# Attention and swish MLP on one core: value phase of batches 0 and 1 pipelined, beta read later, batch 1's attention front moved into pass 2 of slab 0, later norms moved into pass 1

## The chip, the core and the metric

The kernel runs on one core of a Trainium2 chip. The metric is the device time of one execution in microseconds. The engines are called as in the profile: PE (TensorE matmuls; PEld its weight loads), DVE (VectorE), ACT (ScalarE), POOL (GpSimd) and SP (the queue that issues most DMAs). Each engine works through its own instruction queue in order; semaphores tie the queues together.

## What is computed

For 8 batches with 8 heads, 576 positions and 64 channels, a softmax of q over its channels and of k over the positions gives a linear attention; its output goes through an MLP with a swish that has a slope for each hidden channel.

```python
q_s = exp(q - max(q, -1));  q_s /= sum(q_s, -1)
k_s = exp(k - max(k, 2));   k_s /= sum(k_s, 2)
kv  = einsum('bhsd,bhse->bhde', k_s, v)
x   = einsum('bhsd,bhde->bhse', q_s, kv)     # to 4608 tokens x 512
h   = x @ w_in                               # 512 -> 2048
g   = h * sigmoid(beta * h)
out = g @ w_out                              # 2048 -> 512
```

## The kernel before

**Slabs.** The 576 positions of a batch are split into 512 and a remainder of 64. Slab t (0 to 7) is the 512 tokens of batch t; slab 8 is the eight remainders together. For each slab `pass1_tile` runs 16 times: four matmuls of 128x512 (`PS<-XT,WIN`), then ScalarE's Silu with scale beta into `GT`. `pass2_group` then forms the output with 64 matmuls (`PS<-WOUT,GT`), copied to `O2S` and stored. beta's reciprocal is folded into `WOUT` (`scale_wout`).

**Attention of a batch.** It gives `XT`, the left side of pass 1. Head pairs (hp, four of them) are the unit:
- ScalarE's exps: `exp_q` (EQ), `exp_k` (EK), and `exp_kr`, `exp_qr` for the remainders (EKR, EQR).
- `norm_main`: sum of EQ over channels (QS, line 306), reciprocal (QI, 307) and product in place (308); `norm_rem` does it for EQR.
- `t_steps`: four transposes of EQ by a matmul with the identity (line 343), copied to `QT` (363). `tr_steps` does it for EQR (QTR).
- `cast_v` and `cast_vr`: v to bf16 with a column of ones (VB, VR).
- `kv_steps`: EK times VB, five matmuls for a pair, with the sum of EK as column 129; its reciprocal is `RC`, and `kvd` makes `KVD` = product x RC x a mask (380). `ksum` is the sum alone.
- `out_step`: `QT` times `KVD` (`out_mm`), copied to `XT` (417). `outr_steps` does it for the remainders of two batches into `XT8`.

**Order.** The program is written out by hand: `add` appends an operation to its engine's queue and derives its semaphore waits from the tiles and PSUM banks that it touches. In a slab's passes a `tick` runs after each matmul, and `todo` holds steps of the next batch's attention with the tick from which they may go (1 to 64 in pass 1, 65 to 128 in pass 2). PSUM has eight banks: pass 1 rotates through 0 to 2 (HB), pass 2 through 3 and 4 (in slab 0: 3 to 6), attention through 5 to 7 (MB). Batches 0 and 1 have no pass of an earlier slab that could hold all of their attention: `attn_now` runs it at once, for batch 0 in the head of the kernel, for batch 1 between slab 0 and slab 1. There `warm` fills gaps with matmuls whose result nobody reads. Batch 2's attention (`attn_late`) lies in pass 2 of slab 1, batch b's (3 to 7) over both passes of slab b - 1.

**Loads.** SP loads batch 0 (q, beta, k, v); POOL issues eight loads of `WIN`, the first when the last of k has landed; SP then waits for the sixth of them, loads w_out into staging tiles, then batch 1, then batch 2 and so on. POOL also does some norm products and most casts of v.

Of the kernel before, what the change touches and what calls it, by code (L numbers as in the profile page):

```python
# [17 lines left out]
DFF = 2048  # L18
NF = DFF // 128
NM = DM // 128  # L20
# [133 lines left out]
def bass_efficient_attn_shen__then__act_swish_beta_kernel(  # L154
# [12 lines left out]
    with ExitStack() as es:  # L167
# [243 lines left out]
        def out_step(b, hp, pool=MB):  # L411
            i = b % 2

            def one():
                bk = bank(pool)
                out_mm(b, hp, bk)
                add(DVE, lambda e: e.tensor_copy(XT[i][:, hp, :], PS[bk][:, :]),  # L417
                    r=[("ps", bk)], w=[("xt", i, hp)], bank=[bk])
            return [one]
# [34 lines left out]
        def attn(b):  # L454
            s = t_steps(b, (0, 1)) + t_steps(b, (2, 3))
            if b % 2:
                s += tr_steps()
            s += kv_steps(b, (0, 1)) + kv_steps(b, (2, 3))
            for hp in range(NHP):
                s += out_step(b, hp)  # L460
            if b % 2:
                s += outr_steps(b)
            return s

        def attn_late(b):
            s = []
            for hps in ((0, 1), (2, 3)):
                s += t_steps(b, hps) + kv_steps(b, hps)
            for hp in range(NHP):
                s += out_step(b, hp)  # L470
            return s
# [8 lines left out]
        def attn_now(b, pool, wbank, wn, mid):  # L480
            i = b % 2

            def go(steps):
                for s in steps:
                    s()

            def ksum(hp):
                for j in range(5):
                    l, r_, ke, kv, ko = kv_rows(b, hp, j)
                    mm(PS[kb][:, hp:hp + 1], l, r_[:, 128:129], j == 0, j == 4, r=ke + ko,  # L490
                       w=[("ps", kb)], bk=kb)

            exp_q(b)
            for hp in range(NHP):
                norm_main(b, hp, 1, POOL if hp % 2 else DVE)
            mid()
            kb = bank(pool)
            go(t_steps(b, (0,), pool, ACTE))
            warm(wn[0], wbank)
            exp_kr(b, (b % 2,))  # L500
            exp_k(b, 0, 1)
            go(t_steps(b, (1,), pool, ACTE))
            warm(wn[1], wbank)
            exp_k(b, 1, 1)
            ksum(0)
            exp_k(b, 2, 1)
            ksum(1)
            go(t_steps(b, (2,), pool, ACTE))
            warm(wn[2], wbank)
            exp_k(b, 3, 1)  # L510
            ksum(2)
            cast_v(b, 0, ACTE)
            cast_v(b, 1, ACTE)
            go(t_steps(b, (3,), pool, ACTE))
            warm(wn[3], wbank)
            ksum(3)
            cast_v(b, 2, ACTE)
            cast_v(b, 3, ACTE)
            add(DVE, lambda e: e.reciprocal(RC[i][:, :], PS[kb][:, 0:NHP]), r=[("ps", kb)],
                w=[("rc", i, hp) for hp in range(NHP)], bank=[kb])  # L520
            for hp in range(NHP):
                bk = bank(pool)
                for j in range(5):
                    l, r_, ke, kv, ko = kv_rows(b, hp, j)
                    mm(PS[bk][:, 0:128], l, r_[:, 0:128], j == 0, j == 4, r=ke + kv,
                       w=[("ps", bk)], bk=bk)
                kvd(b, hp, bk, 0)
                warm(wn[4], wbank)
                go(out_step(b, hp, pool))
# [24 lines left out]
        HEAD = (1, 2, 3, 4, 5, 6, 7)  # L554
        warm(8, 0)
        bb = bank(HEAD)
# [11 lines left out]
        wgate = []  # L568

        def load_win():  # L570
            for c in range(8):
                a = bass.AP(win_h, 256 * c, [[DFF, 128], [128 * DFF, NM], [1, 256]])
                add(POOL, lambda e, c=c, a=a: e.dma_start(WIN[:, :, 256 * c:256 * c + 256], a),
# [162 lines left out]
```

## Time and profile before

| | |
|---|---|
| median of 3 runs | 328.35 us (327.58 to 328.57) |
| the profiled execution, its own time | 327.24 us |
| its span | 325.4 us |
| PE busy | 293.5 us (90%) |
| ACT, DVE, POOL busy | 166.6, 122.5, 36.6 us |
| DMA | 44.30 MB, mean 136 GB/s |

In a timeline a row is: start and duration in us, engine, line of the kernel, operation, output tile <- input tiles, sizes, count of merged instructions, and in brackets how long the engine had been idle before and what ended that. "SPq" and "POOL ... DMA" rows are issues of a DMA, not its transfer. In the table by stage a row gives the stretch and its length, then each engine's busy time with its count, the granted clock of TensorE, the mean busy share of the DMA engines and GB/s. PEclk on the page is the granted clock in tenths, for 40 equal slices of the span.

### The profile page before, as it was taken

What the parts mean: (1) busy time and instruction counts of PE and PEld (TensorE: products, weight loads), DVE (VectorE), ACT (ScalarE), POOL (GpSimd) and SP (SyncE); (2) the same over time, 40 slices, a digit from 0 to 9 for tenths busy, and PEclk for the clock granted to TensorE, in tenths of its full rate; (3) what the DMA queues carried; (4) which work ended last, traced back from release to release, by engine and by line L of the source; (5) the groups of instructions that cost most, each with busy time, mean ns of one, the idle gap of its engine ahead of it and who ended that gap; (6) DMA issues with size and microseconds to landing.
All of it is one profiled execution on the core that took longest, in us unless ns stands there. A gap on an engine that the chain in (4) does not pass through costs nothing.

```text
span 325.4 us, 3908 instructions
## 1 busy us (share of the span) xinstructions
PE 293.5 (90%) x1569; PEld 139.6 (43%) x1600; DVE 122.5 (38%) x238; ACT 166.6 (51%) x252; POOL 36.6 (11%) x63
## 2 busy tenths in 40 slices
PE   4769992879949999999989989999899999999995
PEld 1334441434425455445535534454355444444442
DVE  1650435251344935910681167107812520010011
ACT  4557407837980569067806780678066018406700
POOL 4460001200073303010200110000000000000000
PEclk9999998799989999999999999999999999999999
DMA  7799999999079952960493000300030002003012
GB/s 213 207 155 255 375 307 286 282 317 254 4 254 250 343 151 69 341 172 2 136 283 131 0 2 2 129 0 2 0 130 2 0 32 99 0 0 131 0 51 78
DMA packets 46098, 44.30 MB, mean 136 GB/s; under 512 B 13808, under 2 KB 42496, under 8 KB 45056
## 3 DMA queue, kind: packets, MB, share of 16 engines
q1 hardware_dynamic: 41536, 41.43, 42.0%
q0 software_dynamic: 4224, 2.10, 5.0%
q10 hardware_dynamic: 320, 0.52, 0.4%
q8 instruction: 12, 0.20, 0.3%
q14 instruction: 6, 0.05, 0.1%
HBM read 36.71 MB, written 9.44 MB: 142 GB/s over the span
## 4 chain that ended last, share of the span: by engine, by line
PE 78%; DVE 13%; ACT 2%; POOL 2%; issue 2%; DMA 1%; SPq 1%; POOLq 0%; DVEq 0%
PE PS L345 76%; DVE QS L306 3%; DVE EQ L308 3%; DVE XT L417 2%; PE PS L343 2%; DVE KVD L380 2%; DMA BT<-in_moe_beta_dram 1%; DVE O2S L604 1%; DVE QI L307 1%; POOL EQ L308 1%; ACT L280 1%; POOL VR L331 1%; SPq L251 1%; ACT EQ L280 0%; ACT O2S L604 0%
## 5 line engine op out<-in xcount | busy, mean ns | idle before, releaser
L599 ACT ACTIVATE GT<-PS,BETA 128x512 bf16<-128x512 f32 x144 | 99.0, 687 | 119.5 <-PE PS L345 119.5
L345 PE MATMUL PS<-WOUT,GT 128*128 128x512 bf16 x564 | 136.9, 382 | 0.5
L345 PE MATMUL PS<-XT,WIN 128*128 128x512 bf16 x560 | 132.5, 379 | 1.1
L345 PEld LDWEIGHTS PS<-WOUT,GT 128*128 128x128 bf16 x576 | 52.6, 98 | 57.5 <-issue 1.9
L345 PEld LDWEIGHTS PS<-XT,WIN 128*128 128x128 bf16 x576 | 50.8, 98 | 54.0 <-DVE XT L417 2.0
L604 DVE COPY O2S<-PS 128x512 f32<-128x512 f32 x34 | 23.2, 686 | 72.4 <-PE PS L345 72.4
L343 PE MATMUL PS<-IDB,EQ 128*128 128x128 bf16 x128 | 25.2, 233 | 9.0 <-DVE EQ L308 6.8
L345 PE MATMUL PS<-VB,EK 128*128 128x129 bf16 (+2 forms) x160 | 26.6, 212 | 4.7 <-POOL VB L323 3.5
L363 DVE COPY QT<-PS 128x1024 bf16<-128x1024 bf16 x12 | 8.3, 690 | 40.2 <-PE PS L343 40.2
L306 DVE TENSOR_REDUCE QS<-EQ 128x8 f32<-128x512 bf16 (+2 forms) x21 | 19.9, 947 | 8.7 <-ACT EQ L280 8.7
L323 POOL CAST VB<-VF 128x512 bf16<-128x512 f32 x24 | 15.4, 642 | 63.8 <-PE PS L345 62.8
L417 DVE CAST XT<-PS 128x512 bf16<-128x512 f32 x32 | 20.4, 683 | 3.9 <-PE PS L345 3.9
L345 PEld LDWEIGHTS PS<-VB,EK 128*128 128x128 bf16 x160 | 13.7, 100 | 16.8 <-POOL VB L323 3.9
L343 PEld LDWEIGHTS PS<-IDB,EQ 128*128 128x128 bf16 x128 | 11.8, 103 | 20.2 <-DVE EQ L308 7.9
L280 ACT ACTIVATE EQ<-QF 128x512 bf16<-128x512 f32 x32 | 17.8, 618 | 3.2 <-DMA QF<-in_q_dram 3.1
L345 PE MATMUL PS<-QT,KVD 128*128 128x512 bf16 x31 | 11.9, 384 | 8.1 <-DVE KVD L380 7.9
L280 ACT ACTIVATE EK<-KF 128x512 bf16<-128x512 f32 x32 | 17.8, 616 | 0.0
L308 DVE TENSOR_TENSOR EQ<-EQ,QI 128x1024 bf16<-128x1024 bf16 (+2 forms) x15 | 16.8, 1119 | 0.5
L345 PE MATMUL PS<-WARM 128*128 128x512 bf16 x37 | 14.5, 508 | 1.3 <-DVE WARM L219 1.2
L400 DVE RECIPROCAL RC<-PS 128x1 f32<-128x1 f32 x24 | 3.9, 161 | 28.6 <-PE PS L345 28.6
L308 POOL TENSOR_TENSOR EQ<-EQ,QI 128x512 bf16<-128x512 bf16 x6 | 6.3, 1042 | 73.7 <-DVE QI L307 73.7
L380 DVE SCALAR_TENSOR_TENSOR KVD<-PS,RC,MASK 128x128 bf16<-128x128 f32 x32 | 11.2, 349 | 2.0 <-PE PS L345 1.0
(53 smaller groups left out, 108.8 us busy)
## 6 DMA issues: line engine op xcount, KB each, us to landing
out_dram<-O2S SPq DMA_DIRECT2D x8, 1024.0 KB, 4.2
QF<-in_q_dram SPq DMA_DIRECT2D x6, 1024.0 KB, 6.8
KF<-in_k_dram SPq DMA_DIRECT2D x6, 1024.0 KB, 8.4
VF<-in_v_dram SPq DMA_DIRECT2D x6, 1024.0 KB, 10.6
WST<-in_moe_w_out_dram SPq DMA_DIRECT2D x3, 1024.0 KB, 8.0
QF<-in_q_dram SPq DMA_DIRECT2D x8, 256.0 KB, 6.7
KF<-in_k_dram SPq DMA_DIRECT2D x8, 256.0 KB, 6.3
VF<-in_v_dram SPq DMA_DIRECT2D x8, 256.0 KB, 6.6
```

What stands on the lines that cost most here:

```text
L280: add(ACTE, lambda e, o=o, a=a: e.activation(o, a, ACT.Exp), r=[(name + "f", i, hp)], w=[("e" + name, i, hp)])
L306: add(DVE, lambda e: e.tensor_reduce(s_, a, AX.X, ALU.add), r=ks, w=[("qs", i, hp0)])
L308: add(eng, lambda e: e.tensor_tensor(a, a, vb, ALU.mult), r=ks + [("qi", i, hp0)], w=ks)
L323: add(eng, lambda e: (e.copy if eng == ACTE else e.tensor_copy)(o, a), r=[("vf", i, hp), ("vone", i)], w=[("vb", i, hp)])
L343: add(PE, lambda e: e.transpose(o, l, r_), r=r, w=w, bank=[bk])
L345: add(PE, lambda e: e.matmul(o, l, r_, start=start, stop=stop), r=r, w=w, bank=[bk])
L363: add(eng, lambda e: (e.copy if eng == ACTE else e.tensor_copy)(o, pb[:, 0:w]), r=[("ps", st["b"])], w=[("qt", i, h) for h in hps], bank=[ ...
L380: add(DVE, lambda e: e.scalar_tensor_tensor(KVD[i][:, hp, :], PS[bk][:, c:c + 128], RC[i][:, hp:hp + 1], MASK[:, :], ALU.mult, ALU.mult), ...
L400: add(DVE, lambda e, s_=s_, h2=h2: e.reciprocal(RC[i][:, h2:h2 + 1], s_), r=[("ps", bk)], w=[("rc", i, h2)], bank=[bk])
L417: add(DVE, lambda e: e.tensor_copy(XT[i][:, hp, :], PS[bk][:, :]), r=[("ps", bk)], w=[("xt", i, hp)], bank=[bk])
L599: add(ACTE, lambda e: e.activation(GT[:, f, :], PS[bk][:, :], ACT.Silu, scale=BETA[:, f:f + 1]), r=[("ps", bk), "beta"], w=[("gt", f)], ba ...
L604: add(eng, lambda e: (e.copy if eng == ACTE else e.tensor_copy)(O2S[t % 2][:, u, :], PS[bk][:, :]), r=[("ps", bk)], w=[("o2", t % 2, u)], ...
```

## The change

`attn_now` is gone. Batch 0's front is written out in the head, with beta's transpose and its four VectorE operations behind the sums. `values_now` lets the value matmuls of head pair hp run ahead of the output matmul of hp - 1, without fillers; in batch 1 ScalarE copies two of the four outputs. Batch 1's exps, norms and casts are queued before pass 2 of slab 0, and its transposes go into pass 2 from tick 112. In slabs 2 to 6 the norms of the next batch are queued at the start of pass 1 instead of between the groups of pass 2, and `attn` starts with the KV steps. Batch 2's v is cast in pass 1 of slab 1, its four norm products are all POOL's. The diff, cut:

```diff
-        def out_step(b, hp, pool=MB):
+        def out_step(b, hp, pool=MB, eng=DVE):
...
-                add(DVE, lambda e: e.tensor_copy(XT[i][:, hp, :], PS[bk][:, :]),
+                add(eng, lambda e: (e.copy if eng == ACTE else e.tensor_copy)(
+                    XT[i][:, hp, :], PS[bk][:, :]),
...
         def attn(b):
-            s = t_steps(b, (0, 1)) + t_steps(b, (2, 3))
+            s = spread(kv_steps(b, (0, 1)) + kv_steps(b, (2, 3)), 8, 36)
+            s += spread(t_steps(b, (0, 1)) + t_steps(b, (2, 3)), 40, 72)
             if b % 2:
-                s += tr_steps()
-            s += kv_steps(b, (0, 1)) + kv_steps(b, (2, 3))
+                s += spread(tr_steps(), 72, 80)
+            x = []
             for hp in range(NHP):
-                s += out_step(b, hp)
+                x += out_step(b, hp)
+            s += spread(x, 84, 108)
             if b % 2:
-                s += outr_steps(b)
+                s += spread(outr_steps(b), 104, 120)
             return s
 
         def attn_late(b):
...
+            s = spread(t_steps(b, (0, 1)), 88, 93) + spread(kv_steps(b, (0, 1)), 94, 99)
+            s += spread(t_steps(b, (2, 3)), 100, 104) + spread(kv_steps(b, (2, 3)), 104, 110)
+            x = []
             for hp in range(NHP):
-                s += out_step(b, hp)
-            return s
+                x += out_step(b, hp, MB, ACTE if hp == 3 else DVE)
+            return s + spread(x, 112, 124)
...
+        def values_now(b, pool, acts):
+            i = b % 2
+            for hp in range(NHP + 1):
+                if hp < NHP:
+                    bk = bank(pool)
+                    for j in range(5):
+                        l, r_, ke, kv, ko = kv_rows(b, hp, j)
+                        mm(PS[bk][:, 0:128], l, r_[:, 0:128], j == 0, j == 4, r=ke + kv,
+                           w=[("ps", bk)], bk=bk)
+                    kvd(b, hp, bk, 0)
+                if hp:
+                    go(out_step(b, hp - 1, pool, ACTE if hp - 1 in acts else DVE))
...
         warm(8, 0)
+        exp_q(0)
+        for hp in range(NHP):
+            norm_main(0, hp, 1, POOL if hp % 2 else DVE)
+        for c in range(8):
+            a = bass.AP(win_h, 256 * c, [[DFF, 128], [128 * DFF, NM], [1, 256]])
+            add(POOL, lambda e, c=c, a=a: e.dma_start(WIN[:, :, 256 * c:256 * c + 256], a),
+                w=[("win", c)], slot=f"win{c}", after=P.writer[("kf", 0, 3)] if c == 0 else ())
...
+        kb = bank(HEAD)
+        go(t_steps(0, (0,), HEAD, ACTE))
+        warm(3, 0)
...
+        ksum(0, 3, kb)
+        ksum_inv(0, kb)
+        warm(2, 0)
         bb = bank(HEAD)
         mm(PS[bb][:, 0:NF], BT[:, :], IDF[:, :], True, True, r=["bt", "idf"], w=[("ps", bb)],
...
-        attn_now(0, HEAD, 0, (3, 3, 3, 2, 1), load_win)
+        values_now(0, HEAD, ())
...
+            if t == 0:
+                kb1 = 7
+                todo = [(112 + 4 * hp, lambda hp=hp: go(t_steps(1, (hp,), NOW[1:], ACTE)))
+                        for hp in range(NHP)]
+            elif t == 1:
+                todo = spread(tr_steps() + outr_steps(1), 24, 52) + attn_late(2)
+            elif t < 7:
+                todo = attn(t + 1)
...
-            if t == 2:
-                norm_main(3, 0, 4)
+            if 2 <= t < 7:
+                norm_main(t + 1, 0, 2)
+                norm_main(t + 1, 2, 2)
+                if t % 2 == 0:
+                    norm_rem()
+            elif t == 1:
                 norm_rem()
+                cast_vr(2)
+                for hp in range(NHP):
+                    cast_v(2, hp)
...
+                exp_q(1)
+                for hp in range(NHP):
+                    norm_main(1, hp, 1, POOL if hp % 2 else DVE)
+                cast_vr(1, (1,))
+                for hp in range(NHP):
+                    cast_v(1, hp)
+                exp_kr(1, (1,))
+                exp_k(1)
                 pass2_group(0, (0, 1, 2, 3), (3, 4, 5, 6), tick)
-                attn_now(1, (7, 0, 1, 2, 5, 6), 3, (0, 0, 6, 6, 1), lambda: cast_vr(1, (1,)))
...
+                for hp in range(NHP):
+                    ksum(1, hp, kb1)
+                    warm(3, 3)
+                ksum_inv(1, kb1)
                 exp_qr()
+                values_now(1, NOW[1:] + (5, 6), (0, 2))
...
-                        norm_main(2, hp, 1, POOL if hp % 2 else DVE)
+                        norm_main(2, hp, 1, POOL)
...
-                if t >= 2 and nb:
-                    if u < 2:
-                        norm_main(nb[0], 2 * u, 2)
-                    elif u == 2 and nb[0] % 2:
-                        norm_rem()
```

What this does to the queues is shown at three places. The first is TensorE's queue where slab 0 ends and batch 1 begins; PS with a number is a PSUM bank, EQ1 to KVD1 are the tiles of batch 1. Before, from the last matmul of pass 2 on:

```order
L345 MATMUL PS6<-WOUT,GT 128x512
L343 MATMUL PS5<-IDB,EQ1 128x128 x4
L343 MATMUL PS6<-IDB,EQ1 128x128 x4
L345 MATMUL PS2<-VB1,EK1 128x1 x4
L345 MATMUL PS2<-VR01,EKR0 128x1
L345 MATMUL PS2<-VB1,EK1 128x1 x4
L345 MATMUL PS2<-VR01,EKR0 128x1
L343 MATMUL PS7<-IDB,EQ1 128x128 x4
L345 MATMUL PS3<-WARM 128x512 x6
```

Of the changed kernel, from the transposes of the third head pair to the first sum:

```order
L343 MATMUL PS2<-IDB,EQ1 128x128 x4
L345 MATMUL PS3<-WOUT,GT 128x512
L345 MATMUL PS4<-WOUT,GT 128x512
L345 MATMUL PS5<-WOUT,GT 128x512
L345 MATMUL PS6<-WOUT,GT 128x512
L343 MATMUL PS0<-IDB,EQ1 128x128 x4
L345 MATMUL PS3<-WOUT,GT 128x512
L345 MATMUL PS4<-WOUT,GT 128x512
L345 MATMUL PS5<-WOUT,GT 128x512
L345 MATMUL PS6<-WOUT,GT 128x512
L345 MATMUL PS7<-VB1,EK1 128x1 x4
L345 MATMUL PS7<-VR01,EKR0 128x1
```

The transposes now stand among pass 2's matmuls. Those of the first head pair went to PS0, two groups earlier, and those of the fourth pair go to PS0 again. ScalarE's queue at this place, in the changed kernel, from batch 1's exps to the first Silu of slab 1:

```order
L280 ACTIVATE EQ1<-QF1 128x2x4x64 x4
L292 ACTIVATE EKR0<-KRF 64x512
L280 ACTIVATE EK1<-KF1 128x2x4x64 x4
L363 COPY QT1<-PS0 128x512
L363 COPY QT1<-PS1 128x512
L363 COPY QT1<-PS2 128x512
L363 COPY QT1<-PS0 128x512
L608 COPY O2S0<-PS4 128x512
L608 COPY O2S0<-PS6 128x512
L296 ACTIVATE EQR<-QRF 128x512
L417 CAST XT1<-PS1 128x512
L417 CAST XT1<-PS0 128x512
```

All QT copies stand behind the last EK, and two XT copies behind EQR; before, QT copies alternated with EK. The second place is the end of batch 1's value phase on TensorE, in the changed kernel:

```order
L345 MATMUL PS6<-VB1,EK1 128x128 x4
L345 MATMUL PS6<-VR01,EKR0 128x128
L345 MATMUL PS0<-QT1,KVD1 128x512
L345 MATMUL PS1<-QT1,KVD1 128x512
L345 MATMUL PS1<-XT1,WIN 128x512 x4
L345 MATMUL PS2<-XT1,WIN 128x512 x4
```

The last output and the first tile of pass 1 share PS1; before, the last output lay in PS2 and the first tile in PS1. The third place is VectorE's queue around pass 2 of slab 2 (batch 3 next). Before, from the first KVDs to the first XT copies:

```order
L380 SCALAR_TENSOR_TENSOR KVD1<-PS7,RC1,MASK 128x128
L604 COPY O2S0<-PS3 128x512
L306 TENSOR_REDUCE QS0<-EQ0 128x16
L307 RECIPROCAL QI0<-QS0 128x16
L308 TENSOR_TENSOR EQ0<-EQ0,QI0 128x1024
L400 RECIPROCAL RC1<-PS5 128x1
L380 SCALAR_TENSOR_TENSOR KVD1<-PS5,RC1,MASK 128x128
L400 RECIPROCAL RC1<-PS5 128x1
L380 SCALAR_TENSOR_TENSOR KVD1<-PS5,RC1,MASK 128x128
L417 CAST XT1<-PS6 128x512
```

Of the changed kernel, from the last copy of slab 1 into slab 2:

```order
L608 COPY O2S1<-PS4 128x512
L306 TENSOR_REDUCE QS1<-EQ1 128x16
L307 RECIPROCAL QI1<-QS1 128x16
L308 TENSOR_TENSOR EQ1<-EQ1,QI1 128x1024
L306 TENSOR_REDUCE QS1<-EQ1 128x16
L307 RECIPROCAL QI1<-QS1 128x16
L308 TENSOR_TENSOR EQ1<-EQ1,QI1 128x1024
L313 TENSOR_REDUCE QRS<-EQR 128x8
L315 RECIPROCAL QRI<-QRS 128x8
L316 TENSOR_TENSOR EQR<-EQR,QRI 128x512
L400 RECIPROCAL RC1<-PS6 128x1
L380 SCALAR_TENSOR_TENSOR KVD1<-PS6,RC1,MASK 128x128
```

The norm block that stood between two groups of KVD in pass 2 now stands ahead of the first KVD, at the start of pass 1, and it is the norm of the very batch whose KVD follow.

109 lines of the change are left out of this document (40 added, 69 removed).

## The prediction

> **What bounds the kernel now.** I began with the page: busy times, the slices with the granted clock, and the chain that ended last.
>
> ```profile
> span 325.4 us, 3908 instructions
> ...
> PEclk9999998799989999999999999999999999999999
> ...
> PE 78%; DVE 13%; ACT 2%; POOL 2%; issue 2%; DMA 1%; SPq 1%; POOLq 0%; DVEq 0%
> ```
>
> TensorE carries 78% of the chain and no matmul of the two MLP passes goes away, so the change can only gain where TensorE waits or runs at a lower clock: the clock sinks in two places, in slices 7 and 8 of 40 (49 to 65 us) and in slice 12 (90 to 98 us). The second view is TensorE's timeline, with the first pass-1 matmul of each slab (`XT,WIN`) as a milestone, and the waits between them in brackets.
>
> ```profile
> 22.45 7.81 PE L345 MATMUL PS<-XT,WIN 128*128 128x512 bf16 x33
> ...
> 54.91 0.61 PE L343 MATMUL PS<-IDB,EQ 128*128 128x128 bf16 x4 [4.36 <-DVE EQ L308]
> ...
> 68.90 3.28 PE L345 MATMUL PS<-XT,WIN 128*128 128x512 bf16 x12
> ...
> 69.84 2.06 PEld L345 LDWEIGHTS PS<-XT,WIN 128*128 128x128 bf16 x11 [0.63 <-DVE XT L417]
> ...
> 95.06 0.23 PE L345 MATMUL PS<-VB,EK 128*128 128x129 bf16 x1 [3.53 <-POOL VB L323]
> ...
> 106.89 6.49 PE L345 MATMUL PS<-XT,WIN 128*128 128x512 bf16 x28
> ...
> 138.54 1.89 PE L345 MATMUL PS<-XT,WIN 128*128 128x512 bf16 x7
> ...
> 165.72 0.39 PE L345 MATMUL PS<-QT,KVD 128*128 128x512 bf16 x1 [1.46 <-DVE KVD L380]
> ...
> 170.69 1.89 PE L345 MATMUL PS<-XT,WIN 128*128 128x512 bf16 x8
> ...
> 203.04 1.67 PE L345 MATMUL PS<-XT,WIN 128*128 128x512 bf16 x7
> ...
> 230.22 0.39 PE L345 MATMUL PS<-QT,KVD 128*128 128x512 bf16 x1 [1.46 <-DVE KVD L380]
> ...
> 235.20 1.89 PE L345 MATMUL PS<-XT,WIN 128*128 128x512 bf16 x8
> ...
> 266.17 13.98 PE L345 MATMUL PS<-XT,WIN 128*128 128x512 bf16 x62
> ```
>
> The slabs take 46.45, 37.99, 31.65, 32.15, 32.35, 32.16 and 30.97 us (slabs 0 to 6). Slab 6 carries a whole odd batch of attention and no norms in its pass 2: 30.97 us is the measure of a slab that hardly waits. The third view is a table by stage.
>
> ```profile
> 13.70:16.50 2.80, 2.56 (x35) 1.68 (x35) 0.17 (x2) 2.70 (x6) 2.65 (x3) 1.00 0.02 7
> 22.40:50.50 28.10, 27.80 (x126) 12.36 (x127) 7.95 (x18) 11.34 (x17) 0.00 (x0) 1.00 1.15 305
> 50.50:54.90 4.40, 0.05 (x1) 0.00 (x0) 2.36 (x6) 4.20 (x7) 0.00 (x0) 0.98 1.04 250
> 54.90:64.40 9.50, 6.92 (x54) 3.76 (x56) 3.68 (x9) 7.77 (x14) 2.69 (x3) 0.65 1.10 305
> 235.20:266.17 30.97, 30.81 (x178) 15.39 (x180) 9.35 (x20) 11.00 (x16) 0.00 (x0) 1.00 0.08 35
> ```
>
> The columns are PE, PEld, DVE, ACT, POOL, clock, DMA share, GB/s. Slab 0's two passes have no gap (27.80 of 28.10). Behind them TensorE stands still for 4.4 us and then works 9.5 us at a mean clock of 0.65. The DMA engines idle early for 2.8 us (share 0.02), and are full in slab 0 and up to 64.40 (1.04 to 1.15; transfers that wait in parallel make it more than 1).
>
> **Term 1, the head: about 3 us earlier, but worth nothing by itself.** VectorE's first reduction stood behind the beta operations, which waited for a load and a transpose.
>
> ```profile
> 7.25 0.63 ACT L280 ACTIVATE EQ<-QF 128x512 bf16<-128x512 f32 x1 [0.53 <-DMA QF<-in_q_dram]
> ...
> 7.59 0.28 PE L343 MATMUL PS<-IDF,BT 16*128 16x16 f32 x1 [2.80 <-DMA BT<-in_moe_beta_dram]
> ...
> 8.70 0.63 DVE L306 TENSOR_REDUCE QS<-EQ 128x8 f32<-128x512 bf16 x1
> ...
> 10.75 1.49 PE L345 MATMUL PS<-WARM 128*128 128x512 bf16 x3
> ...
> 10.99 0.59 ACT L363 COPY QT<-PS 128x512 bf16<-128x512 bf16 x1 [3.11 <-PE PS L343]
> ...
> 14.56 0.81 PE L345 MATMUL PS<-WARM 128*128 128x512 bf16 x3
> ...
> 18.35 0.69 DVE L417 CAST XT<-PS 128x512 bf16<-128x512 f32 x1 [0.48 <-PE PS L345]
> ...
> 18.96 0.34 DVE L380 SCALAR_TENSOR_TENSOR KVD<-PS,RC,MASK 128x128 bf16<-128x128 f32 x1
> ...
> 19.35 0.39 PE L345 MATMUL PS<-QT,KVD 128*128 128x512 bf16 x1 [0.55 <-DVE KVD L380]
> ```
>
> With beta later, the first transposes come at about 6 instead of 10.35 us, and ScalarE's 3.11 us gap closes. From the end of its fourth exp (7.88) it owes four QT copies (0.59), EKR and four EK (0.63 each, as EQ): 5.5 us, so EK ends near 13.6 with a short wait for the last transposes, about 2.3 us earlier. The last sum, two fillers and beta's four VectorE operations (0.8 us lay between its transpose's end at 7.87 and 8.70) then stand ahead of the first KVD: about 15.8. In the value phase a head pair cost 1.43 us, because the output matmul waited 0.55 us for its KVD. Pipelined, VectorE (0.34 + 0.69) sets about 1.1 us a pair. First pass-1 matmul: near 19.5, not 22.45.
>
> **Term 2, up to the first matmuls of slab 1: 10.1 us.** What decides here is the DMA stream.
>
> ```profile
> SPq L544 <- DMA WIN<-in_moe_w_in_dram: 17.9, 1, 17.9
> ...
> 14.83 1.73 POOL L573 DMA_DIRECT2D WIN<-in_moe_w_in_dram  x2
> ...
> 42.37 1.36 SPq L251 DMA_DIRECT2D KF<-in_k_dram  x2
> DMA to landing us min/median/max: 7.1/7.5/9.1
> ...
> 48.34 1.79 SPq L258 DMA_DIRECT2D QRF<-in_q_dram  x2
> ...
> L323 POOL CAST VB<-VF 128x512 bf16<-128x512 f32 x24 | 15.4, 642 | 63.8 <-PE PS L345 62.8
> ```
>
> The row of times to landing is that of batch 1's four K loads.
>
> WIN's issue at 14.83 stood behind POOL's last norm product. That product moves with the head's norms (4.4 us) to an end near 10.6, so WIN starts when batch 0's last K load lands; ScalarE read it well before 14, I take about 11.3, which is 3.5 us earlier. Batch 0's V keeps the engines busy until 13.7, so the stream gains just the 2.8 us of idle time. SP's later queue hangs on WIN (17.9 us of waiting), then w_out, then batch 1's Q and K at full DMA load: I shift it all by 2.8 (bounds 0 and 3.5). The last K load of batch 1, issued near 43.05 and landing 7.1 to 7.5 later, arrives at about 50.3 before, 47.5 after.
>
> From there, in ScalarE's order: the last EK 48.15, the first QT copy 48.75. The fourth head pair's transposes go to the same PSUM bank as the first's (PS0, in the order above), so they wait for that copy, inside pass 2. By TensorE's own work (124 matmuls of 0.217 and three groups of 0.2 behind 19.5) they would come at about 47.0. So pass 2 ends at 48.8 + 0.2 + 4 × 0.217 = 49.9, 1.8 us later than TensorE could: of the head's 3 us that much is hidden, and with no gain there at all slab 1 would start only 1.1 later. Then four sums with three filler matmuls each (0.41 + 0.65): values start at 54.2. Eight groups of TensorE (0.61 and 0.39) with the KVD waits end with the last output matmul at 58.3. Slab 1's first tile takes the bank of that last output (PS1), so it waits for the XT copy (0.69): 59.05, its fourth matmul 59.7. Before, the fourth matmul came at 69.84 after its own wait. Gain 10.1. No wait is over 2 us here, so I expect no low clock.
>
> Hidden costs: POOL's four VB casts (0.64 each, ScalarE's before) end near 52.6, before the values. ScalarE's two XT copies stand behind EQR, whose two loads were issued by 50.13 and land near 56 by the same 7 us, now 53.3; so they are free from 53.9, and the first is due at 55.9. Such a cast on ScalarE isn't in the trace; its QT copy (0.59) and VectorE's cast (0.69) bound it, I take 0.6. Were EQR as late as before, it would hold the first XT copy by 0.8.
>
> **Term 3, the rest of slab 1: 6.7 us.** From the fourth matmul to slab 2 took 37.05 us. The trace shows the 3.53 us wait for POOL's VB cast, a lower clock behind it (the 8 of slice 12), 0.53 us for a norm product, and small waits for QTR and XT. Now VR and VB of batch 2 are cast in pass 1, where POOL is idle, and the transposes come 24 matmuls into pass 2.
>
> ```profile
> 84.65 1.28 ACT L280 ACT_TABLE_LOAD   x1
> ...
> 89.17 1.04 POOL L308 TENSOR_TENSOR EQ<-EQ,QI 128x512 bf16<-128x512 bf16 x1 [29.05 <-DVE QI L307]
> ```
>
> With the start of pass 2 as zero (83.74 before): table load until 2.2, first exp 2.85, sum and reciprocal 3.8, four POOL products of 1.04 done at 4.95, 6.0, 7.05, 8.1. Transposes of pairs 0 and 1 need them at 5.2 and 6.1, those of 2 and 3 at 8.8: no wait over 0.1. With slab 6 as measure, 30.97 - 0.65 = 30.3: gain 6.7 (if POOL is 1 us late, 5.7).
>
> **Term 4, slabs 2 to 5: 5.0 us.** Their norms leave pass 2, where a 2.7 us block on VectorE held KVD.
>
> ```profile
> 127.22 1.21 DVE L306 TENSOR_REDUCE QS<-EQ 128x16 f32<-128x1024 bf16 x1
> ...
> 128.75 1.22 DVE L308 TENSOR_TENSOR EQ<-EQ,QI 128x1024 bf16<-128x1024 bf16 x1
> ```
>
> Odd batches (slabs 2, 4) come down to 30.97: 0.68 and 1.38. Even ones (3, 5) lose the same 1.46 us wait each. Now the block, 2 × 2.7 + 1.6 with the remainder, opens pass 1 and holds that batch's first KVD until about 9 us into it. Nothing of TensorE needs this before tick 56 (14 us), when the transposes reuse the KVD's bank. So the cover is 5 us.
>
> **The sum.** 10.1 + 6.7 + 5.0 = 21.8: a span of 303.6. Around the span the profiled run has 1.84 us (327.24), so 305.4. The median of the runs shown, 328.35, is 1.1 higher and the lowest 0.3 higher: I add 0.6 and forecast **306.0 us**.
>
> **Rivals.**
> - *The stream does not shift*: WIN's early start is given back among the V packets. Batch 1's K lands at 50.3 again, everything from slab 1 on is 2.8 later: 308.8. For it: the share of 1.15 in slab 0 says that DMA has no slack. Against: the idle 2.8 us are plainly there.
> - *The norms are late again*, on VectorE in pass 1 or on POOL in slab 1: term 4 is given back, 311.0.
> - *The clock stays low in the head*: TensorE now works in short bursts from 6 us on. After the restart at 10.35 us three fillers took 1.49 us, and only those of 14.56 us 0.81. If the bursts don't count, the value phase costs 0.75 more a pair (3.0) and pass 1 starts with 3.4 us at half speed (1.7). Of these 4.7 us, 1.8 hide behind the K wait: 308.9. The Trainium skill, page "TensorE: Matmul & The Clock Gate", Part 1, "What's actually happening", has this rule: an idle window of about 3.4 us brings half rate, and about 3.4 us of sustained work is needed to leave it. The trace agrees after the 4.36 us gap (0.65 in that stage); it doesn't show whether bursts are enough.
> - *Slower than before*: the moved block on VectorE. If it ran so slowly that KVD came after 14 us of pass 1, each further microsecond would be lost in five slabs (2 to 6). From 18.4 us on, 4.4 lost in each, the whole 21.8 is gone. The block would have to take over twice its 7 us; against it, nothing in the two rows above points to such a stretch.
>
> **How the numbers follow.** Forecast 0.62 (own range 303 to 308); no shift 0.12; late norms 0.12; low clock 0.09; slower 0.03; the change doesn't do what it says, within 0.3% of before, 0.02 (0.3% is what a measurement of this kernel can tell from no change). Only the last two are not faster: 0.95, 0.02, 0.03. The low end takes the 3.5 us shift (0.7), transposes not held by the copy (1.1), the profiled run's own frame (0.6) and slab 1 without its small waits (0.6): 303.0. The high end takes the late norms: 311.0.
>
> **What would show it.** First `XT,WIN` near 19.5, slab 1's near 59, slab 2's near 90, with 31 us for each of slabs 2 to 6; WIN issued near 11.3; the fourth transposes of batch 1 waiting for a QT copy; no clock below 1 after the head. A TensorE wait on KVD or EQ in pass 1 of slabs 2 to 6 would prove terms 3 and 4 wrong; slab 1 starting at 62 would prove the shift wrong.

## The result and the profile after

The changed kernel takes 303.09 us, the median of four runs (301.78 to 305.95), against 327.97 for the kernel before on the same chip (326.95 to 328.57). The ratio is 0.9256 with an interval of 0.9177 to 0.9335: 24.9 us less. The forecast was 306.0 with a range of 303.0 to 311.0: the measured time lies inside, 0.1 above its low end. The profiled run took 304.23 us, with a span of 302.4.

From the page of the changed kernel: the span, the granted clock in 40 slices, and the chain that ended last.

```profile
span 302.4 us, 3926 instructions
...
PEclk9799999999999999999999999999999999999999
...
PE 81%; DMA 9%; SPq 4%; DVE 2%; POOL 1%; issue 1%; ACT 0%
```

The two low stretches behind slab 0 (slices 7, 8 and 12 of before) are gone; one new dip, in slice 2, lies in the head. VectorE leaves the chain (13% to 2%), and DMA enters it (1% to 9%).

The table by stage of the changed kernel, cut at the first pass-1 matmul of each slab. The columns are PE, PEld, DVE, ACT, POOL (busy us and instructions), clock, DMA share, GB/s.

```profile
17.60:58.06 40.46, 35.05 (x201) 16.33 (x199) 16.35 (x38) 23.61 (x36) 6.00 (x9) 1.00 1.14 285
58.06:89.21 31.15, 31.14 (x181) 15.28 (x181) 12.61 (x29) 23.57 (x39) 10.31 (x14) 1.00 1.09 301
89.21:120.18 30.97, 30.97 (x181) 15.41 (x180) 16.93 (x29) 18.93 (x28) 7.35 (x10) 1.00 0.86 258
120.18:150.70 30.52, 30.52 (x170) 14.95 (x168) 13.83 (x24) 18.35 (x27) 4.68 (x6) 1.00 0.51 154
150.70:181.67 30.97, 30.97 (x181) 15.39 (x180) 16.61 (x29) 18.35 (x27) 3.50 (x4) 1.00 0.13 44
181.67:212.19 30.52, 30.52 (x170) 14.93 (x169) 13.83 (x24) 18.35 (x27) 0.00 (x0) 1.00 0.08 35
```

In slabs 2 to 6 the PE column equals the length of the slab (2 to 5 are shown): TensorE does not wait there. The 23.0 us of span come from three places: slab 1's start is 10.84 earlier (68.90 to 58.06: 4.85 in the head and 5.99 in slab 0), slab 1 is 6.84 shorter (37.99 to 31.15), and slabs 2 to 5 together 5.33 (128.31 to 122.98). Slab 6 and what follows did not change.

Where TensorE still waits, on its timeline (start, busy us, and in brackets the wait and what ended it):

```profile
15.08 0.39 PE L345 MATMUL PS<-QT,KVD 128*128 128x512 bf16 x1 [0.42 <-DVE KVD L380]
...
17.37 0.39 PE L345 MATMUL PS<-QT,KVD 128*128 128x512 bf16 x1 [0.47 <-DVE KVD L380]
17.60 0.81 PE L345 MATMUL PS<-XT,WIN 128*128 128x512 bf16 x3
...
49.59 0.38 PE L343 MATMUL PS<-IDB,EQ 128*128 128x128 bf16 x4 [2.14 <-ACT QT L363]
...
50.68 0.24 PE L345 MATMUL PS<-VB,EK 128*128 128x1 bf16 x4
...
53.96 0.39 PE L345 MATMUL PS<-VB,EK 128*128 128x128 bf16 x4
...
58.06 2.12 PE L345 MATMUL PS<-XT,WIN 128*128 128x512 bf16 x9 [0.79 <-DVE XT L417]
```

The fourth head pair's transposes of batch 1 wait 2.14 us for the copy of the first pair's, and slab 1's first tile waits for the last XT copy, as forecast. What holds the copy is seen in the chain of waits of the changed kernel (start, us, what), which leads back through the loads:

```profile
16.20 7.53 DMA WIN<-in_moe_w_in_dram
...
40.22 8.11 DMA KF<-in_k_dram
...
48.35 0.63 ACT EK L280
48.98 0.48 ACT QT L363
```

So slab 0 ends when batch 1's last K has landed (48.33) and ScalarE has made its exp and the first QT copy. The chain's WIN transfer goes back to its issue on POOL's timeline:

```profile
11.71 1.73 POOL L545 DMA_DIRECT2D WIN<-in_moe_w_in_dram  x2 [1.29 <-DMA KF<-in_k_dram]
```

It stands 3.1 us earlier than before (14.83), and now waits for batch 0's last K load, not for a norm product.

### The profile page after: what moved, and what is told of

Read it like the earlier page. It is cut to its first block, busy times and chain, and to the rows that moved or that the text cites. A ratio compares the mean times of both kernels' runs of the same rounds, so it can differ in the third digit from the quotient of the medians.

```text
span 302.4 us, 3926 instructions
## 1 busy us (share of the span) xinstructions
PE 287.6 (95%) x1592; PEld 138.3 (46%) x1592; DVE 122.1 (40%) x236; ACT 166.6 (55%) x251; POOL 43.8 (14%) x69
## 4 chain that ended last, share of the span: by engine, by line
PE 81%; DMA 9%; SPq 4%; DVE 2%; POOL 1%; issue 1%; ACT 0%
PE PS L345 79%; DMA KF<-in_k_dram 5%; SPq L251 3%; DMA WIN<-in_moe_w_in_dram 2%; PE PS L343 2%; DMA WST<-in_moe_w_out_dram 2%; POOL WIN L545 1%; DVE WOUT L532 1%; SPq L258 1%; DVE XT L417 0%; DVE KVD L380 0%; DVE O2S L608 0%; ACT EK L280 0%; POOL VR L331 0%; ACT QT L363 0%
## 5 line engine op out<-in xcount | busy, mean ns | idle before, releaser
L345 PE MATMUL PS<-XT,WIN 128*128 128x512 bf16 x576 | 135.5, 379 | 0.9 <-DVE XT L417 0.9
L345 PE MATMUL PS<-WOUT,GT 128*128 128x512 bf16 x576 | 134.7, 379 | 0.0
L343 PE MATMUL PS<-IDB,EQ 128*128 128x128 bf16 x128 | 23.8, 225 | 6.0 <-DVE EQ L308 2.2
L345 PE MATMUL PS<-VB,EK 128*128 128x129 bf16 (+2 forms) x160 | 25.3, 209 | 1.0 <-ACT EK L280 1.0
L323 POOL CAST VB<-VF 128x512 bf16<-128x512 f32 x28 | 20.5, 731 | 34.9 <-PE PS L345 31.7
L280 ACT ACTIVATE EQ<-QF 128x512 bf16<-128x512 f32 x32 | 18.1, 620 | 10.6 <-DMA QF<-in_q_dram 10.4
L306 DVE TENSOR_REDUCE QS<-EQ 128x8 f32<-128x512 bf16 (+1 forms) x22 | 20.1, 912 | 7.2 <-ACT EQ L280 7.2
L345 PEld LDWEIGHTS PS<-VB,EK 128*128 128x128 bf16 x160 | 13.5, 98 | 10.1 <-ACT EK L280 2.1
L308 DVE TENSOR_TENSOR EQ<-EQ,QI 128x1024 bf16<-128x1024 bf16 (+1 forms) x14 | 15.7, 1123 | 0.5
L308 POOL TENSOR_TENSOR EQ<-EQ,QI 128x512 bf16<-128x512 bf16 x8 | 8.3, 1042 | 37.0 <-DVE QI L307 36.8
L345 PE MATMUL PS<-WARM 128*128 128x512 bf16 x31 | 11.0, 482 | 1.2 <-DVE WARM L219 1.2
L532 DVE TENSOR_SCALAR WOUT<-WST,RB 128x512 bf16<-128x512 f32 x12 | 5.0, 481 | 15.4 <-DMA WST<-in_moe_w_out_dram 15.4
```

The source lines that it names most:

```text
L280: add(ACTE, lambda e, o=o, a=a: e.activation(o, a, ACT.Exp), r=[(name + "f", i, hp)], w=[("e" + name, i, hp)])
L306: add(DVE, lambda e: e.tensor_reduce(s_, a, AX.X, ALU.add), r=ks, w=[("qs", i, hp0)])
L308: add(eng, lambda e: e.tensor_tensor(a, a, vb, ALU.mult), r=ks + [("qi", i, hp0)], w=ks)
L323: add(eng, lambda e: (e.copy if eng == ACTE else e.tensor_copy)(o, a), r=[("vf", i, hp), ("vone", i)], w=[("vb", i, hp)])
L343: add(PE, lambda e: e.transpose(o, l, r_), r=r, w=w, bank=[bk])
L345: add(PE, lambda e: e.matmul(o, l, r_, start=start, stop=stop), r=r, w=w, bank=[bk])
```

## The experiments

Each kernel is the changed one with the edit shown, and ran beside the kernel before on the same chip. A step of 0.001 in the ratio is 0.33 us. Effects are given against the ratio of the unchanged yardstick, which ran once, on one of the chips, so a difference of two ratios has an interval of its own, about 1.7 us to either side (worked out from the two intervals; 2.3 for the old step order):

> The changed kernel again, on the chip on which the next three run, as their yardstick. Expected: a median near 303 us and a spread of some 4 us between runs. Theory of the spread: the fourth transposes of batch 1 wait for a DMA-timed copy inside pass 2, so the moment of the last K landing decides, and with a longer wait a half clock follows. Rival: the spread belongs to the chip and the kernel before would show it too in this job.

Measured: 303.22 us, ratio 0.9250 [0.9212, 0.9288], six runs from 302.50 to 304.96. Its span was 300.8, 1.6 less than in the first profile. ScalarE's and TensorE's rows say where the 1.6 is from; first those of the changed kernel's first profile, then of this run.

```profile
48.88 2.03 ACT L363 COPY QT<-PS 128x512 bf16<-128x512 bf16 x4
...
54.75 0.63 ACT L296 ACTIVATE EQR<-QRF 128x512 bf16<-128x512 f32 x1 [2.87 <-DMA QRF<-in_q_dram]
55.29 0.57 ACT L417 CAST XT<-PS 128x512 bf16<-128x512 f32 x1
```

```profile
47.28 2.03 ACT L363 COPY QT<-PS 128x512 bf16<-128x512 bf16 x4
...
56.47 0.82 PE L345 MATMUL PS<-XT,WIN 128*128 128x512 bf16 x3 [0.79 <-DVE XT L417]
```

The QT copies began 1.60 earlier and slab 1 1.59 earlier (58.06 to 56.47). From the copies to slab 1 lie 9.18 and 9.19 us, from slab 1 to the end of the span 244.3 both times. In the two profiled runs the difference is all in when K lands. For the timed runs the rival stands: beside the yardstick the kernel before spread by 2.9 us, the yardstick itself by 2.5.

**Is the head worth anything?** Two kernels move slab 0's start without touching the loads. The first adds 12 unread filler matmuls, the second removes those between the steps of the head:

```diff
         values_now(0, HEAD, ())
+        warm(12, 0)
```

> Twelve filler matmuls (2.6 us at full clock) ahead of pass 1 of slab 0, nothing else. Theory (the head's gain is hidden behind the DMA stream; the trace has 3.7 us of waits in the last quarter of pass 2 of slab 0): slab 1 starts within 0.5 us of the changed kernel, the time within 0.5 us. Rival (the head is on the path): 2.6 us slower.

```diff
         go(t_steps(0, (0,), HEAD, ACTE))
-        warm(3, 0)
         go(t_steps(0, (1,), HEAD, ACTE))
-        warm(2, 0)
...
         go(t_steps(0, (2,), HEAD, ACTE))
-        warm(2, 0)
...
         ksum(0, 0, kb)
-        warm(2, 0)
...
         ksum_inv(0, kb)
-        warm(2, 0)
```

> All fillers of the head behind the first eight are left out, so that TensorE has long gaps there and comes cold into pass 1. Rival of the prediction (low clock in the head): value phase and the first 3.4 us of pass 1 of slab 0 at half clock, slab 0 up to 4.7 us later than its 17.6 to 18.2. Theory (the waits of 3 to 4 us in pass 2 of slab 0 take this up): the time stays within 1 us of the changed kernel all the same. If the head is not hidden: 2 to 4 us slower.

Measured: 303.35 us, 0.9242 [0.9210, 0.9274], and 303.23 us, 0.9231 [0.9195, 0.9266]: no difference from 0.9250 in either. The timeline of the kernel with more fillers:

```profile
20.27 4.05 PE L345 MATMUL PS<-XT,WIN 128*128 128x512 bf16 x18
...
56.32 2.98 PE L345 MATMUL PS<-XT,WIN 128*128 128x512 bf16 x13 [0.79 <-DVE XT L417]
```

Slab 0 starts 2.6 us late (the fillers began at 17.68) and slab 1 on time: the wait for the QT copy takes it up. In the other kernel the clock stayed low through the whole value phase (its table by stage, then its TensorE rows):

```profile
7.80:11.20 3.40, 1.51 (x13) 0.90 (x13) 1.57 (x4) 3.11 (x8) 1.12 (x2) 0.51 1.09 271
11.20:14.50 3.30, 1.89 (x24) 1.46 (x24) 0.83 (x5) 2.77 (x6) 2.31 (x4) 0.50 0.93 257
14.50:18.20 3.70, 3.59 (x21) 2.08 (x21) 3.03 (x8) 2.82 (x5) 3.70 (x7) 0.51 1.25 158
```

```profile
15.33 0.61 PE L345 MATMUL PS<-QT,KVD 128*128 128x512 bf16 x1
...
16.27 0.63 PE L345 MATMUL PS<-QT,KVD 128*128 128x512 bf16 x1
...
18.22 0.81 PE L345 MATMUL PS<-XT,WIN 128*128 128x512 bf16 x3
```

At a clock of 0.51 a head pair took 0.94 us (15.33 to 16.27), with TensorE itself busy for 3.59 of the last 3.70 us, and pass 1 began at the full clock (three matmuls in 0.81 us, as at 17.60). Slab 0 began 0.6 us later than at 17.60, not the 4.7 that the rival of the low clock charged.

**Is it the shifted stream?** This kernel lets WIN start only behind batch 0's last V load.

```diff
-                w=[("win", c)], slot=f"win{c}", after=P.writer[("kf", 0, 3)] if c == 0 else ())
+                w=[("win", c)], slot=f"win{c}", after=P.writer[("vf", 0, 3)] if c == 0 else ())
```

> The first w_in load waits for the last V load of batch 0 (landing near 14.6 us) instead of the last K load (11.4). Theory (the DMA stream decides when slab 1 starts): w_in, w_out and batch 1 all land about 3 us later, slab 1 starts 2.5 to 3.5 us later, the whole 2.5 to 3.5 us slower, and perhaps a half clock on top where the wait in pass 2 passes 3 us. Rival (TensorE's own head decides): no change, as the head's matmuls are as early as before.

Measured: 305.79 us, 0.9317 [0.9282, 0.9352]: 2.2 us slower. Slab 1 starts at 58.74, 2.27 later than in the yardstick. The edit has a side effect in the head, on TensorE (the last row here is ScalarE's, its first QT copy of batch 1):

```profile
16.97 0.29 PE L345 MATMUL PS<-VR,EKR 128*128 128x128 bf16 x1 [2.23 <-POOL VR L331]
...
20.65 0.81 PE L345 MATMUL PS<-XT,WIN 128*128 128x512 bf16 x3
...
50.27 0.38 PE L343 MATMUL PS<-IDB,EQ 128*128 128x128 bf16 x4 [1.52 <-ACT QT L363]
...
49.56 2.03 ACT L363 COPY QT<-PS 128x512 bf16<-128x512 bf16 x4
```

POOL's cast of VR stands behind the WIN issues, so slab 0 starts late too. But the fourth transposes still wait 1.52 us for the QT copy, so slab 0's late start sets nothing, and the QT copies, which no matmul of slab 0 holds up, begin 2.28 us later than the yardstick's 47.28, with WIN issued 2.7 us later (14.56 against 11.88). So the 2.2 us are the stream's, a little less than expected. The head's norms pay by what they let POOL issue earlier.

**Pipelining the values.** Here the value phases of both batches run one pair after the other, with a filler, as before, and all XT copies are VectorE's again; the two are undone together:

```diff
...
-            for hp in range(NHP + 1):
-                if hp < NHP:
...
-                if hp:
-                    go(out_step(b, hp - 1, pool, ACTE if hp - 1 in acts else DVE))
+            for hp in range(NHP):
...
+                kvd(b, hp, bk, 0)
+                warm(1, 0 if b == 0 else 3)
+                go(out_step(b, hp, pool))
```

> The value phase of batches 0 and 1 goes back to one head pair after the other with a filler between, all XT copies on VectorE. Theory (the pipelining is worth its 0.4 us a pair in batch 1, the head's part is hidden): 1.6 to 2.2 us slower than the changed kernel. Rival (batch 1's values wait for DMA-timed casts of v anyway): under 0.7 us slower.

Measured: 305.69 us, 0.9317 [0.9283, 0.9351]: 2.2 us slower. The fourth transposes and batch 1's value phase in its timeline:

```profile
47.70 0.39 PE L343 MATMUL PS<-IDB,EQ 128*128 128x128 bf16 x4
...
52.07 0.39 PE L345 MATMUL PS<-VB,EK 128*128 128x128 bf16 x4
...
58.44 1.90 PE L345 MATMUL PS<-XT,WIN 128*128 128x512 bf16 x8 [0.79 <-DVE XT L417]
```

The value phase takes 6.37 us (52.07 to 58.44), pipelined 4.10 (53.96 to 58.06): 2.27 us more. But here batch 0's share is not all hidden. K came early in this profile (QT copies from 46.20), and the fourth transposes, at 47.70, wait for no copy: slab 0 had started late (19.96), and TensorE's own work sets its end. Slab 1 starts 12.24 us behind the copies, 3.06 more than the 9.18 of the changed kernel; 2.27 of that are batch 1's values, the other 0.8 the head's. So the head is hidden only as long as K lands late enough. The timed difference alone, 2.2 us with its interval of 1.7, does not exclude the rival's 0.7; the trace does, for the value phase.

**Slab 1.** Batch 2's part of slab 1 is put back as before: steps spread over ticks 86 to 126, VectorE sharing the norms, the V casts behind the exps.

```diff
-            s = spread(t_steps(b, (0, 1)), 88, 93) + spread(kv_steps(b, (0, 1)), 94, 99)
...
+            for hps in ((0, 1), (2, 3)):
+                s += t_steps(b, hps) + kv_steps(b, hps)
...
+            return spread(s, 86, 126)
...
-                cast_vr(2)
-                for hp in range(NHP):
-                    cast_v(2, hp)
...
-                        norm_main(2, hp, 1, POOL)
+                        norm_main(2, hp, 1, POOL if hp % 2 else DVE)
...
```

> Only batch 2's part in slab 1 goes back: its v is cast in pass 2 again, its norm products alternate between VectorE and POOL, its steps start at tick 86 with KV close behind. Theory (term 3): slab 1 takes about 37 us instead of 31.2, with the wait for POOL's VB cast and a half clock behind it: 5.5 to 6.5 us slower. Rival (a part of term 3 came from batch 1's earlier finish, which gives the loads of batch 2 more time): 3 us slower or less.

Measured: 309.91 us, 0.9459 [0.9427, 0.9491]: 6.9 us slower, so the rival with 3 us or less is out. TensorE's wait and the low stretch that follows, from its timeline and its table by stage:

```profile
81.59 0.29 PE L345 MATMUL PS<-VB,EK 128*128 128x129 bf16 x1 [3.52 <-POOL VB L323]
```

```profile
55.96:94.69 38.73, 34.65 (x180) 16.26 (x181) 13.87 (x31) 23.44 (x38) 11.16 (x17) 0.91 1.02 283
80.79:87.60 6.81, 6.00 (x24) 2.97 (x25) 1.48 (x5) 2.45 (x4) 4.91 (x9) 0.50 0.71 228
```

One wait of 3.52 us brings 6.8 us at a clock of 0.50, from 80.79 on. The first 0.8 of these still belong to the wait (it ends at 81.59); the other 6.0 us of work would take about 3.0 at the full clock. Wait and low clock together cost about 6.5 us of the 7.58 by which slab 1 is longer (38.73 against 31.15). The price is not fixed: in the kernel before, the same wait (3.53 us) was followed by about 3.4 us at half clock (95.7 to 99.1), half as long. The edit puts back three things at once, the V casts, POOL's norm products and the ticks; no run tells which of them removes the wait.

**Slabs 2 to 6: norms or step order?** Three kernels undo the one, the other, and both.

Norms back between the groups of pass 2, the KV steps still first:

```diff
-            if 2 <= t < 7:
-                norm_main(t + 1, 0, 2)
-                norm_main(t + 1, 2, 2)
...
+            if t == 2:
+                norm_main(3, 0, 4)
+                norm_rem()
...
+                if t >= 2 and nb:
+                    if u < 2:
+                        norm_main(nb[0], 2 * u, 2)
...
```

> Only the norms of slabs 2 to 6 go back between the groups of pass 2; the KV steps stay early in pass 1. Theory A, as predicted (the norm block's leaving pass 2 is worth the 5.0 us): 5 us slower than the changed kernel, KVD waits of about 1.4 us in three slabs. Theory B (the early KV steps alone took KVD out of the block's way, since in pass 2 only XT copies are left behind it): within 0.5 us of the changed kernel and no TensorE wait on KVD after slab 1.

The order of the steps back (transposes first), the norms still in pass 1:

```diff
-            s = spread(kv_steps(b, (0, 1)) + kv_steps(b, (2, 3)), 8, 36)
-            s += spread(t_steps(b, (0, 1)) + t_steps(b, (2, 3)), 40, 72)
+            s = t_steps(b, (0, 1)) + t_steps(b, (2, 3))
...
+            s += kv_steps(b, (0, 1)) + kv_steps(b, (2, 3))
...
+            return spread(s, 28 if b == 3 else 8, 112)
```

> Only the order of the attention steps in slabs 2 to 6 goes back (transposes from tick 8, in slab 2 from 28, KV late); the norms stay at the start of pass 1. Theory (the norm block in pass 1 costs nothing only because its first user comes at tick 40): the transposes now wait 2 to 5 us in each of slabs 3 to 6 for EQ, with half clocks behind the longer waits: 10 to 20 us slower than the changed kernel. Rival (the place of the norms decides, not the order of the steps): within 1 us of it.

Both edits together:

> In slabs 2 to 6 both go back: the norms into pass 2 and the attention steps into their old order (transposes first, KV late). Theory (the two belong together; either move alone takes the norm block out from between KV and output): 5.0 us slower than the changed kernel, with waits for KVD of about 1.4 us in three slabs, as in the kernel before. Rival (something else of the change made these slabs faster): less than 2 us slower.

Measured, in this order: 303.95 us, 0.9258 [0.9221, 0.9294]; 309.68 us, 0.9457 [0.9397, 0.9517]; 307.99 us, 0.9393 [0.9367, 0.9420]. Against the yardstick that is +0.3 (not to be told from nothing), +6.8 and +4.7 us. Slabs 3 and 4 in the tables by stage of the three, in the same order:

```profile
118.56:149.08 30.52, 30.52 (x169) 14.94 (x168) 14.71 (x27) 18.34 (x27) 3.68 (x6) 1.00 0.50 153
149.08:180.06 30.98, 30.98 (x182) 15.39 (x181) 14.68 (x27) 18.35 (x27) 2.46 (x4) 1.00 0.14 44
```

```profile
118.19:150.61 32.42, 30.69 (x170) 14.86 (x168) 13.78 (x24) 18.35 (x27) 3.67 (x6) 1.00 0.50 147
150.61:183.49 32.88, 31.15 (x182) 15.31 (x180) 15.97 (x29) 18.35 (x27) 2.46 (x4) 1.00 0.11 38
```

```profile
119.39:151.55 32.16, 30.69 (x169) 14.86 (x168) 14.94 (x27) 18.35 (x27) 3.67 (x6) 1.00 0.49 148
151.55:183.90 32.35, 31.15 (x181) 15.27 (x180) 14.38 (x26) 18.34 (x27) 2.46 (x4) 1.00 0.08 34
```

With the norms back in pass 2 nothing is lost as long as the KV steps have left it. With both back, slabs 3 and 4 take 32.16 and 32.35 us, as before (32.15 and 32.35), and the wait on KVD returns:

```profile
146.58 0.39 PE L345 MATMUL PS<-QT,KVD 128*128 128x512 bf16 x1 [1.47 <-DVE KVD L380]
```

With the norms in pass 1 and the transposes there too, TensorE meets the block on VectorE directly; this is its timeline in that kernel:

```profile
121.81 0.23 PE L343 MATMUL PS<-IDB,EQ 128*128 128x128 bf16 x1 [1.73 <-DVE EQ L308]
```

That happens once in each of slabs 3 to 6, at 1.90 us a slab, the clock staying at 1.00. So the step order carries this term, to within the interval of the +0.3. The norms' move alone would have made the kernel slower: with the old step order, slab 2 to the end of the span takes 220.8 us with the norms in pass 1 and 218.3 with them in pass 2 (the ratios, 2.1 us apart, have an interval as wide).

**What holds slab 0's end now?** The wait at 49.59 is on a shared PSUM bank. With a fourth bank for the transposes:

```diff
-                kb1 = 7
-                todo = [(112 + 4 * hp, lambda hp=hp: go(t_steps(1, (hp,), NOW[1:], ACTE)))
+                kb1 = 2
+                todo = [(112 + 4 * hp, lambda hp=hp: go(t_steps(1, (hp,), NOW, ACTE)))
```

> Batch 1's transposes rotate through four PSUM banks (2, 7, 0, 1) instead of three, the sums take bank 2, whose copy ScalarE makes first. So the fourth transposes no longer wait for the first QT copy and thus for the last K load. Theory A (that wait sets slab 1's start): pass 2 of slab 0 ends 1.5 to 2 us earlier and the whole is 1.5 to 2 us faster. Theory B (ScalarE's EQR, whose load lands near 54.7 us, stands ahead of the XT copies and takes its place): pass 2 ends earlier, but the first XT copy comes where it was, under 0.5 us of gain.

Measured: 302.52 us, 0.9232 [0.9194, 0.9270], not to be told from the yardstick. In this profile K came late (QT copies at 48.07) and slab 1 started 8.45 us behind the copies, at 56.52, instead of 9.19: some 0.7 us are gained. The transposes no longer wait for the copy (0.35 us of that wait is left, at the first sum), but another wait has come, on ScalarE and TensorE of that kernel:

```profile
54.18 0.63 ACT L296 ACTIVATE EQR<-QRF 128x512 bf16<-128x512 f32 x1 [3.11 <-DMA QRF<-in_q_dram]
...
54.72 1.05 ACT L417 CAST XT<-PS 128x512 bf16<-128x512 f32 x2
...
55.34 0.39 PE L345 MATMUL PS<-QT,KVD 128*128 128x512 bf16 x1 [1.16 <-ACT XT L417]
```

The last output matmul waits 1.16 us there, where the changed kernel waits 0.55 for KVD, and the value phase takes 4.73 us (51.79 to 56.52) instead of 4.10: 0.6 us are given back. ScalarE's two XT copies stand in its queue behind EQR, which waits 3.11 us for a load that the value phase doesn't need. So EQR moves behind them as well:

```diff
-                exp_qr()
                 values_now(1, NOW[1:] + (5, 6), (0, 2))
+                exp_qr()
```

> As the run with four banks, and EQR is queued behind the XT copies on ScalarE. Theory A: no more than with the banks alone. Theory B: now the gain appears, 1.5 to 2 us faster than the changed kernel; V's last load (53.2 us) and its cast are the next limit.

And, on top of both, one filler instead of three behind each of the four sums:

```diff
-                    warm(3, 3)
+                    warm(1, 3)
```

> Four banks, EQR behind the XT copies, and one filler matmul instead of three behind each of batch 1's four sums. Theory (behind the mended copies TensorE's own queue sets slab 1's start): 1.7 us of fillers gone, of which the last V cast leaves 1.0 to 1.5: faster than the run with EQR moved by that much, some 300 us. Rival (the fillers hold the clock up): a half clock after slab 0 and no gain, or a loss.

Measured: 301.25 us, 0.9202 [0.9167, 0.9236], and 300.83 us, 0.9174 [0.9141, 0.9207]. Slab 1 starts at 54.96 and 53.56, with K early in both profiles (QT copies at 46.60 and 46.30), so that part of this is not the edits'. The timeline of the last:

```profile
49.45 0.38 PE L345 MATMUL PS<-VB,EK 128*128 128x128 bf16 x4 [0.61 <-ACT O2S L608]
...
53.56 2.76 PE L345 MATMUL PS<-XT,WIN 128*128 128x512 bf16 x12 [0.79 <-DVE XT L417]
```

The last version is faster than the changed kernel too: its interval lies below the yardstick's, 2.5 us by the ratios. The first of the two steps (0.9202) overlaps with the yardstick, so its 1.6 us are not settled; nor is the second's gain over the first, 0.9 us by the ratios, where 1.0 to 1.5 were expected. The clock stays at 1.00 in this value phase, so the rival of the fillers did not come. The next limit is not V's cast but a copy of O2S that holds a bank for 0.61 us.

## Why the prediction was right

The forecast time was 2.9 us too high, and its path was the measured one. The sum gave a span of 303.6 against 302.4; the rest is the median, which was taken 0.6 above the profiled run and lay 1.1 below it. That the sum met this profile so closely is in part luck: in the yardstick K landed 1.6 us earlier, and the span was 300.8.

- **Term 1, the head.** "Worth nothing by itself" holds where K lands late: moving slab 0's start by 2.6 us changed nothing. With K early, 0.8 us of a late head came through (the values in sequence). The size was off: 17.60, not 19.5. The first output matmul came at 15.08, where KVD was expected from 15.8 on, and the four of them took 0.76 us apart (15.08 to 17.37), not 1.1.
- **Term 2, slab 1's start, 10.1 forecast, 10.84 measured** by the first matmul; by the fourth, which the prediction counts, it is 11.1 (69.84 to 58.7). The mechanism is the one named: WIN's issue moved to 11.71 (forecast 11.3), K's landing sets the QT copies, and these the fourth transposes. Two sizes erred against each other in the first profile. K landed later there than the forecast 47.5 (48.33; in the yardstick the copies began 1.6 earlier, so that there both erred the same way and slab 1's start gained 12.4). The path behind it was shorter: the four sums with their fillers took 3.28 us (50.68 to 53.96), where the matmul times had been added up to 4.24 although they overlap, and the values took 4.10, not 4.85. The wait for the copy was 2.14 us, over the 2 us that the prediction allowed; the clock stayed at 1.00 all the same. Of the term, the runs take apart the stream (2.2) and the values (2.3). The largest part, batch 1's front in pass 2, was never put back alone; for it there is only the trace, in which the 4.36 us wait and the low clock behind it are gone.
- **Term 3, slab 1: 6.7 forecast, 6.84 measured** (6.5 from the fourth matmul on, as the prediction counts), and 6.9 by putting it back. The 3.52 us wait for VB and the low clock behind it are the most of it.
- **Term 4, slabs 2 to 5: 5.0 forecast, 5.33 measured,** 4.7 by putting both parts back. The size was right, the cause only half named. The prediction gave the gain to the norms that leave pass 2; the runs give it to the KV steps that leave it. Either keeps KVD clear of the block, but only with the KV steps first does TensorE not need the normed EQ at once.
- **The rivals.** *No shift of the stream* is excluded by the late WIN: issued 2.7 us later, it cost 2.2, where the rival charged 2.8 for the lost shift. *Late norms* did not happen here; the kernel with the old step order shows what it would have been, once 1.73 us a slab. There my expectation had the place right, but charged far more. *Low clock in the head*: a dip did occur, and its price of 4.7 us was wrong. At the full clock VectorE's KVD and XT copies set the pace of the value phase, 0.76 us a pair; at half clock TensorE set it, at 0.94, only 0.2 more; and by then TensorE was busy enough for pass 1 to begin at the full clock. *Slower* and *no change* are excluded by the ratio.
- **Named as hidden, and nearly not.** The prediction gave ScalarE 2.0 us between the end of EQR (53.9) and the first XT copy (55.9). EQR came at 54.75, after 2.87 us of waiting for its load, and the first XT copy followed right behind it at 55.29 (the rows above): nothing was left of the 2.0. With one bank more EQR held the copies.

What stays open is how much of the spread between timed runs (4.2 us in the first measurement, 2.5 in the yardstick, beside which the kernel before has 2.9) is K's landing. The profiled runs show that landing; the timed runs have no trace.

## What to carry to other kernels

When a wait is removed, look for the one that ends next in the same stretch: here a K load, a PSUM bank shared with an earlier copy, and an exp queued ahead of copies that did not need it lay so close together that removing the bank's wait (1.65 us in the yardstick) gained some 0.7 us. When a change moves both a producer's block and its consumer's steps, undo each alone: one may carry the whole gain, and the other may be harmless only beside it. Where transfers decide, an earlier start of other work is worth what it lets the queue issue earlier; its own microseconds count only once the transfers come early enough.

## What the runs showed of the hardware that was not expected

In the profiled runs the landing of one load set the whole time to a tenth of a microsecond. In five profiled kernels that differ elsewhere (the changed one twice, the one with the norms back, and the two with other fillers in the head) the QT copies began between 47.12 and 48.88, slab 1 always 9.18 to 9.20 later, and the span ended 244.3 to 244.4 behind that.

By the clock column a low stretch lasted about 3.4 us, or two or three times that: 3.4 in the head of the changed kernel (7.7 to 11.2), 6.8 in slab 1 put back, 10.3 without the head's fillers (7.7 to 18.1). This is the changed kernel's table by stage in the head:

```profile
4.30:7.80 3.50, 1.38 (x9) 0.45 (x7) 3.33 (x8) 2.00 (x4) 1.90 (x5) 1.00 0.89 258
7.80:11.20 3.40, 3.29 (x19) 1.67 (x19) 1.40 (x3) 2.84 (x7) 1.10 (x2) 0.50 1.11 284
11.20:14.50 3.30, 2.29 (x34) 1.58 (x32) 0.64 (x4) 3.13 (x6) 2.79 (x4) 1.00 1.11 288
```

Behind a stretch with 1.38 us of matmuls the clock is 0.50 for 3.4 us; TensorE is busy for 3.29 of these and gets the full clock back. Without the head's fillers it was busy for 1.51 of 3.40 and 1.89 of 3.30 us, and the clock stayed at half until it had been busy for 3.59 of 3.70 (the table above). The Trainium skill, page "TensorE: Matmul & The Clock Gate", Part 1, "What's actually happening", asks for about 3.4 us of sustained work to leave the half rate. The trace agrees: in these stretches short bursts did not suffice, which the prediction had left open.

Where the low stretches fall is not set by the program alone, and the clock column misses the first of them. It says 1.00 from the start, but in the changed kernel the first eight fillers, at 1.19, took 3.46 us, 0.43 each, against 0.22 at 17.68 in the kernel with twelve more fillers. Two other profiles of the same head show it longer: three fillers at 6.4 took 1.49 us there, where the first profile has 0.81 at 6.19. By such durations the yardstick is at half rate up to about 10.5 and again from 13.7 to 17.1, the kernel with twelve more fillers up to about 9 and not again.

The half rate cost little in the head, 0.6 us of slab 0's start, because at the full clock TensorE had been waiting for VectorE there.
